# Convolution and locality-gated mixture of experts on one core: weight and token loads in shorter runs, rows that carry 64 channels twice, and one ScalarE copy less a block

## The chip, the cores and the metric

The kernel runs on one core of a Trainium2 chip. The core has a matrix engine (TensorE, "PE" in the profile, with its weight loads as "PEld"), a vector engine (VectorE, "DVE"), an activation engine (ScalarE, "ACT"), a general engine (GpSimd, "POOL") and an engine that mostly issues transfers (SyncE, "SP"). Sixteen DMA engines move data between the main memory (HBM) and the on-chip memory; the profile lists their queues as q0 (transfers that GpSimd issues, which follow index lists), q1 (transfers that SyncE issues) and q8 and q14 (instructions). The metric is the device time of one execution in microseconds (us), as the median of several runs.

## The reference, cut to what matters

Inputs are x with 8 sequences of 3584 tokens of 192 channels, 8 heads with 7 taps, a gate for 8 experts, a local gate, and for each expert two weight matrices (192x1024 and 1024x192). Everything is float32.

```python
w = softmax(weight)                                  # 8 heads x 7 taps
x[b, s] = sum_k w[h, k] * x_pad[b, s + k]            # channels of head h, k = 0..6
logits = x @ w_gate                                  # 8 experts
local = sigmoid(x @ w_local)
for each batch b, for s in order:
    e = argmax(logits[b, s]) if s == 0 or local[b, s] < 0.5 else prev_e
    prev_e = e
    out[b, s] = softmax(logits[b, s])[e] * (relu(x[b, s] @ w1[e]) @ w2[e])
```

So each of the 28,672 tokens goes through the two matrices of one expert, and which expert can depend on the token before.

## The kernel before, in words

The tokens are worked on in 16 parts of 1792 tokens (14 tokens on each of 128 partitions). For every part the kernel computes the convolution, the logits, the expert of each token and the token's place in a table of slots in main memory, sorted by expert. A row of a token in that table (`slots`, one row of `DG` floats) holds the probability, the token's number, its 192 channels and the number once more; that is 195 floats or 780 bytes. GpSimd scatters the rows there (`put`, line 767: one instruction for 128 rows, lines 773 to 776), and once enough rows of an expert stand there, they are read back in blocks.

A block is one or two units of 128 tokens of one expert. There are three kinds, listed in line 882: kind 0 has 35 blocks of one unit, taken while few parts are routed; kind 1 has 87 blocks of two units; kind 2 has 20 blocks of one unit at the end, and two spare ones that run only if needed. The main loop over the blocks (from line 1137) does for block i:

- `ensure` (line 1089) issues the reading of the rows of blocks up to i + 3 (`load_rows`, line 906, tile `xg`, six buffers), and works on the routing of further parts if their rows are not there yet.
- `weights` (line 1100) issues the loads of the expert's two matrices up to block i + 3 (`load_w`, line 896, tile `wb`, four buffers, 1536 KB: 12,288 bytes on each partition). Blocks 0 to 3 load them in three pieces of 512 KB, the others in one DMA.
- `hidden` (line 951) multiplies the first matrix: 48 matmuls with 64 rows each, two row halves of TensorE side by side, into four accumulators `hps`; ScalarE applies the ReLU.
- `turn` (line 927) transposes the rows of block i + 1 on TensorE: 64x128 and, for the last 64 channels, 64x64 pieces. ScalarE then makes four copies from `xps` to `xT`, since each row half of TensorE needs three groups of 64 channels on its own partitions; the last group has to reach both halves.
- `step` (line 1036) puts operations of the next parts' convolution (`conv`, line 366; VectorE and ScalarE) and routing (`route`, line 600) between those of the block, by a budget of time. Routing begins with `logits` (line 564).
- `output` (line 972) multiplies the second matrix, scales on ScalarE and VectorE, and GpSimd scatters the 128 results of each unit to `out` (line 995).

The order on each engine is written out by hand: the program's order is the engines' order. SyncE issues rows, weights and parts' tokens (`load_x`, line 114, tile `x_sb`: 1920 KB, 15,360 bytes on each partition) in one order; a transfer that waits for a buffer, for scatters or for its semaphore holds up those behind it. GpSimd has the scatters to `slots` and to `out` in one order.

The first two parts go another way (`wide`, line 195, and `wide_route`): their convolution is done on TensorE, and GpSimd copies the last 64 channels of the rows aside (`again`, line 221) for the transposes. The rows of the first two blocks are picked on TensorE with a matrix of zeros and ones, `hot` (`hots`, `gather`, `gathered`, lines 546 to 562).

A convolved part lies in `y_sb`, of which there are four buffers (`row_tile`, line 363); `again` and the scatters read it.

Of the kernel before, what the change touches and what calls it, by code (L numbers as in the profile page):

```python
# [8 lines left out]
F32 = mybir.dt.float32  # L9
# [8 lines left out]
P = 128  # L18
B, S, D = 8, 3584, 192
# [4 lines left out]
UT = 128  # L24
# [5 lines left out]
NB = 16  # L30
TB = PT // NB
NI = TB + HALO
NH = NB // 2
NX = NT + HALO
DR = P // 2
# [3 lines left out]
KT = BT // P  # L39
# [18 lines left out]
HALF = 0.5  # L58
FULL = {0: ONE[0], HALF: _sure(PT + PT // 2, UT), **{g: ONE[g] for g in range(1, NPART)}}
REST = NU - ONE[-1] - 2 * TWO[-1]  # L60
DG = 3 + D
Y0 = 2
IX = DG - 1
Q = 32
DQ = D // Q
TQ = (NT + 3) // 4
WA = F * KD // 2
WB = FK * D
# [13 lines left out]
def kernel(  # L82
# [10 lines left out]
    nc = tc.nc  # L93
    cst = ctx.enter_context(tc.tile_pool(name="cst", bufs=1))
# [15 lines left out]

    slots = dram.tile([(DUMMY + 1 + E) * UT, DG], F32, name="slots")


    def load_x(g):
        x_sb = xs.tile([P, NX, D], F32, name="x_sb")
        src = x[g // PER]
        win = bass.AP(tensor=src.tensor, offset=src.offset + g % PER * PT * D,
                      ap=[[NT * D, P], [1, NX * D]])
        nc.sync.dma_start(out=x_sb.rearrange("p t d -> p (t d)"), in_=win)
        return x_sb  # L120

    def load_b(g):
# [15 lines left out]
    with tc.tile_pool(name="scr", bufs=1) as scr:  # L138
        w = scr.tile([1, H, KC], F32, name="w")
# [50 lines left out]
    def z_tile():  # L190
        return yt.tile([P, 3 * NH * TB + NB * DR], F32, name="z")
# [3 lines left out]
    def wide(g, xv, y_sb, both):  # L195
# [25 lines left out]
        def again(half):  # L221
            bs = slice(half * NH, (half + 1) * NH)
            nc.gpsimd.tensor_copy(yr[:, bs, :], y_sb[:TB, bs, Y0 + P:Y0 + D])

        def turned(half, qs):
            at = half * 3 * NH // 2
# [83 lines left out]
    rows = cst.tile([Q, 2, Q], F32, name="rows")  # L310
# [22 lines left out]

    pad = cst.tile([P, DG], F32, name="pad")
    nc.gpsimd.memset(pad, 0.0)
# [17 lines left out]
    def halves():  # L353
        return [(half, slice(half * DR, (half + 1) * DR)) for half in range(2)]

    def turn_half(to, src, half):

        rows = slice(half * DR, (half + 1) * DR)
        nc.tensor.transpose(to, src[rows], identity=ident[rows, rows])  # L359
# [3 lines left out]
    def row_tile():  # L363
        return ys.tile([P, NB, DG], F32, name="y_sb")

# [192 lines left out]
    def gathered(ps):  # L558
        xg = xp.tile([P, KT, DG], F32, name="xg")
        nc.scalar.copy(xg[:, 0, :Y0 + D], ps[:, :Y0 + D])  # L560
        nc.scalar.copy(xg.bitcast(I32)[:, 0, IX:], ps[:, 1:2])
        return xg

    def logits(g, y_sb):

        z = z_tile()[:, :NT * D].rearrange("p (t d) -> p t d", d=D)
        for t in range(0, NT, TQ):
            u = min(t + TQ, NT)
            nc.vector.transpose(z[:, t:u, :], y_sb[:, t:u, Y0:Y0 + D])  # L569
            yield 0.2 * (u - t)  # L570
        yield "hop"


        lps = [hps_p.tile([P, TQ * Q], F32, name="hps") for half in range(2)]
        begin = [min(TQ * j, NT - TQ) for j in range(4)]
        for b in range(DQ):
            for j in range(4):
                for half, rows in halves():
                    nc.tensor.matmul(lps[half][Q * j:Q * j + Q, :], lhsT=wgq[rows, b, :],  # L579
                                     rhs=z[rows, begin[j]:begin[j] + TQ, b * Q:(b + 1) * Q],  # L580
                                     start=(b == 0), stop=(b == DQ - 1))
        ls = sm.tile([P, 2, TQ * Q], F32, name="ls", bufs=1)
        for half in range(2):
            nc.scalar.copy(ls[:, half, :], lps[half])  # L584
        yield "hop"
        lq = sm.tile([P, 2 * TQ, Q], F32, name="lq", bufs=1)
        nc.vector.transpose(lq.rearrange("p t e -> p (t e)"), ls.rearrange("p h x -> p (h x)"))  # L587
        yield 0.4
        lt = sm.tile([P, NT + 2, E + 1], F32, name="lt")
        for r in range(4):  # L590
            for j in range(4):
                t, u = TQ * j, min(TQ * (j + 1), NT)
                at = r // 2 * TQ + t - begin[j]
                e0 = r % 2 * (E + 1)
                nc.vector.tensor_copy(lt[Q * r:Q * r + Q, t:u, :],  # L595
                                      lq[Q * j:Q * j + Q, at:at + u - t, e0:e0 + E + 1])
                yield 0.12
        return lt
# [285 lines left out]
    blocks = [(0, 1, i, next(g for g in FULL if i < FULL[g])) for i in range(ONE[-1])]  # L884
# [3 lines left out]
    AHEAD = 3  # L888
# [7 lines left out]
    def load_w(i):  # L896
        e = entry(i, 1, E - 1)
        wb = wp.tile([P, WA + WB], F32, name="wb")
        src = w12[bass.ds(e, 1)].rearrange("o p x -> (o p) x")

        step = WA + WB if i > AHEAD else (WA + WB) // 3
        for x0 in range(0, WA + WB, step):
            nc.sync.dma_start(out=wb[:, x0:x0 + step], in_=src[:, x0:x0 + step])
        return wb

    def load_rows(i):
        n, group = blocks[i][1], blocks[i][3]
        r = entry(i, 0, DUMMY + 1 - n)
        xg = xp.tile([P, KT, DG], F32, name="xg")
        get = nc.sync.dma_start(  # L910
# [16 lines left out]
    def turn(n, xg):  # L927


        xps = xps_p.tile([P, 2, 512], F32, name="xps")  # L930
        at = xps[:, :, :BT].rearrange("p h (d k s) -> p h d k s", d=2, k=KT)
        for d in range(2):
            for k in range(n):
                src = xg[:, k, Y0 + d * P:Y0 + min((d + 1) * P, D)]
                for half in range(2):
                    turn_half(at[:src.shape[1], half, d, k, :], src, half)
        xT = tp.tile([P, KD, BT], F32, name="xT")
        to = xT.rearrange("p d (k h s) -> p h d k s", k=KT, h=2)
        (_, up), (_, low) = halves()
        for dst, ds, src, d0 in ((slice(0, P), (0, 1), slice(0, P), 0), (low, (1, 3), up, 0),  # L940
                                 (up, (1, 2), up, 1), (up, (2, 3), low, 0)):
            a = to[dst, :, ds[0]:ds[1]]
            b = at[src, :, d0:d0 + ds[1] - ds[0]]
            if n == KT:
                a, b = [v.rearrange("p h d k s -> p h (d k) s") for v in (a, b)]
            else:
                a, b = [v[:, :, :, 0, :] for v in (a, b)]
            copied = nc.scalar.copy(a, b)  # L948
        return xT, copied

    def hidden(n, wb, xT, shares=(1, 1)):
# [100 lines left out]
                time -= c  # L1052

    ya, yb = row_tile(), row_tile()
    hot = cst.tile([P, 2, NB, UT], F32, name="hot")
    wide0 = wide(0, x_in.pop(0), ya, True)
    wide1 = wide(1, x_in.pop(1), yb, False)

# [69 lines left out]
    xT, _ = turn(blocks[0][1], xgs[0])  # L1128
# [8 lines left out]
    for i, (_, n, _, _) in enumerate(blocks):  # L1137
# [6 lines left out]
        if i + 1 < len(blocks):  # L1144
            xT, copied = turn(blocks[i + 1][1], xgs[i + 1])
# [6 lines left out]
    kind, _, at, group = spare[0]  # L1152
    any_left = nc.values_load(tabi[kind, group][at:at + 1, 0:1], min_val=0, max_val=DUMMY,  # L1153
                              skip_runtime_bounds_check_because="an entry of the table")
    with tc.If(any_left < DUMMY):
        for block in spare:
            blocks.append(block)
            i = len(blocks) - 1
            n = block[1]
            xg = load_rows(i)  # L1160
            wb = load_w(i)
            xT, _ = turn(n, xg)
# [3 lines left out]
def _w1_layout(np, w1):  # L1166


    w = w1.reshape(E, KD, DR, 2, F // 2).transpose(0, 3, 2, 1, 4)
    w = np.stack([w[:, 0][:, :, [0, 2, 1]], w[:, 1][:, :, [1, 0, 2]]], 1)  # L1170
    return w.reshape(E, P, KD * F // 2)


# [57 lines left out]
```

## Time and profile before

| What | Value |
|---|---|
| median of 3 runs | 1331.93 us (1331.38 to 1332.31) |
| the profiled execution | 1331.38 us, of it 1329.7 from the first to the last instruction |
| TensorE matmul busy | 1306.9 us, 98% of the span |
| VectorE, ScalarE, GpSimd busy | 778.8, 624.2, 477.9 us |
| moved by DMA | 325.29 MB, 245 GB/s over the span |
| start of block 0, 2, 35 (first block of two units), 122 (first of kind 2) on TensorE | 45.96, 65.23, 264.70, 1213.45 us |

Lines of the profile name the line of the kernel, the engine, the operation, the tile written and the tiles read, the shape and the count; then the busy time, the mean time of one in ns, the engine's idle time before them and what ended that. "issue" there is time for which the profile shows nothing that the engine waited for. In the view by windows the columns are the stretch (us from the span's start), its length, then the busy time of PE, PEld, DVE, ACT and POOL with the number of instructions, the granted clock, the DMA engines' busy share and GB/s. In an engine's order of time the columns are the start, the length, the group and, in brackets, idle time. The slices of the page cut the span into 40 equal parts of 33.2 us, each digit a busy share in tenths.

### The profile page before, as it was taken

How to read it: one execution, taken by the hardware profiler on the slowest of the kernel's cores; microseconds unless marked ns; L12 is line 12 of the kernel's file. 1: busy time of each engine (PE TensorE's matmuls, PEld its weight loads, DVE VectorE, ACT ScalarE, POOL GpSimd, SP SyncE). 2: the span in 40 equal slices, each digit the busy share in tenths (PEclk: the TensorE clock that was granted, in tenths of full speed). 3: DMA queues.
4: the chain of work that ended last, by engine and by line, in shares of the span. 5: the costliest groups of instructions: out<-in, count | busy, mean ns of one | idle time of the engine just before them, and what ended most of it. 6: DMA issues, size and time to landing. Idle time of an engine off the chain costs nothing. (4 is left out here: it accounts for less than half of the span.)

```text
span 1329.7 us, 41356 instructions
## 1 busy us (share of the span) xinstructions
PE 1306.9 (98%) x16682; PEld 1256.0 (94%) x16682; DVE 778.8 (59%) x2434; ACT 624.2 (47%) x1571; POOL 477.9 (36%) x520
## 2 busy tenths in 40 slices
PE   9799999999999999999999999999999999999997
PEld 7799999999999999999999999999999999999997
DVE  5879898977878787878777878786610000000000
ACT  5345555544444544444444444444444444444553
POOL 3445343524243434343434343434344211211111
PEclk9999999999999999999999999999999999999999
DMA  4799999967575757575757575756565555556883
GB/s 184 273 336 386 365 355 353 377 227 264 185 275 185 286 188 280 195 266 191 276 180 276 191 276 191 274 191 217 194 216 207 189 180 188 188 188 232 313 324 123
DMA packets 67298, 325.29 MB, mean 245 GB/s; under 512 B 12576, under 2 KB 38103, under 8 KB 47650
## 3 DMA queue, kind: packets, MB, share of 16 engines
q1 hardware_dynamic: 44784, 277.41, 58.3%
q0 software_dynamic: 22320, 45.22, 9.2%
q8 instruction: 133, 2.18, 0.6%
q14 instruction: 59, 0.48, 0.1%
q10 hardware_dynamic: 2, 0.00, 0.0%
HBM read 277.29 MB, written 45.77 MB: 243 GB/s over the span
## 5 line engine op out<-in xcount | busy, mean ns | idle before, releaser
L979 PE MATMUL yps<-wb,hT 64*128 64x192 f32 x7328 | 641.0, 326 | 5.4 <-DVE o_sb L991 2.7
L962 PE MATMUL hps<-xT,wb 64*128 64x256 f32 (+1 forms) x6816 | 634.1, 336 | 3.3 <-issue 1.8
L979 PEld LDWEIGHTS yps<-wb,hT 64*128 64x128 f32 x7328 | 602.2, 187 | 11.8 <-issue 7.7
L962 PEld LDWEIGHTS hps<-xT,wb 64*128 64x128 f32 x6816 | 581.2, 187 | 33.5 <-issue 4.1
L995 POOL DMA_INDIRECT out_dram<-o_sb,xg x229 | 232.1, 1014 | 604.7 <-DVE o_sb L991 543.7
L967 ACT ACTIVATE hT<-hps 128x512 f32<-128x512 f32 (+1 forms) x568 | 261.6, 512 | 364.4 <-PE hps L962 246.9
L387 DVE SCALAR_TENSOR_TENSOR y_sb<-x_sb,c,y_sb 128x336 f32<-128x336 f32 x672 | 376.3, 570 | 18.4 <-ACT y_sb L377 0.3
L991 DVE SCALAR_TENSOR_TENSOR o_sb<-yps,xg,o_sb 128x192 f32<-128x192 f32 x229 | 87.5, 414 | 468.0 <-ACT o_sb L987 457.7
L774 POOL DMA_INDIRECT slots<-y_sb,posi x228 | 229.0, 1004 | 216.2 <-ACT xT L948 118.8
L987 ACT ACTIVATE o_sb<-yps,xg 128x192 f32<-128x192 f32 x229 | 86.8, 417 | 288.9 <-PE yps L979 283.3
L948 ACT COPY xT<-xps 64x256 f32<-64x256 f32 (+4 forms) x568 | 210.7, 371 | 13.4 <-PE yps L979 1.8
L377 ACT ACTIVATE y_sb<-x_sb,c 128x336 f32<-128x336 f32 x112 | 63.7, 580 | 0.0
L359 PEld LDWEIGHTS xps<-ident,xg 64*128 64x128 f32 (+1 forms) x916 | 54.1, 124 | 5.8
L359 PE MATMUL xps<-ident,xg 64*128 64x64 f32 (+1 forms) x916 | 57.5, 217 | 0.0
L569 DVE STREAM_TRANSPOSE z<-y_sb 128x768 f32<-128x768 f32 (+1 forms) x56 | 45.4, 853 | 0.4
L595 DVE COPY lt<-lq 32x36 f32<-32x36 f32 x224 | 40.7, 182 | 3.5
L579 PE MATMUL hps<-z,wg 64*32 64x128 f32 x1344 | 25.3, 272 | 1.9 <-issue 1.7
L579 PEld LDWEIGHTS hps<-z,wg 64*32 64x32 f32 x1344 | 19.4, 105 | 5.3 <-issue 4.1
L587 DVE STREAM_TRANSPOSE lq<-ls 128x256 f32<-128x256 f32 x14 | 6.2, 441 | 14.2 <-ACT ls L584 14.2
L671 DVE COPY bk<-so_far 1x32 f32<-1x32 f32 x56 | 12.7, 228 | 0.7
L555 PE MATMUL yps<-y_sb,hot 112*128 112x194 f32 x64 | 11.5, 332 | 1.4 <-DVE hot L549 1.4
L555 PEld LDWEIGHTS yps<-y_sb,hot 112*128 112x128 f32 x64 | 10.4, 189 | 2.1 <-DVE hot L549 1.6
(236 smaller groups left out, 358.5 us busy)
## 6 DMA issues: line engine op xcount, KB each, us to landing
wb<-in_w_dram SPq DMA_DIRECT2D x138, 1536.0 KB
x_sb<-in_x_dram SPq DMA_DIRECT2D x14, 1920.0 KB
xg<-slots SPq DMA_DIRECT2D x87, 195.0 KB
wb<-in_w_dram SPq DMA_DIRECT2D x12, 512.0 KB
xg<-slots SPq DMA_DIRECT2D x53, 97.5 KB
out_dram<-o_sb,xg POOLq DMA_INDIRECT x229
slots<-y_sb,posi POOLq DMA_INDIRECT x228
x_sb<-in_xb_dram SPq DMA_DIRECT2D x4, 768.0 KB
```

What stands on the lines that cost most here:

```text
L359: nc.tensor.transpose(to, src[rows], identity=ident[rows, rows])
L377: nc.scalar.activation(cols(h), chans(h, 0), Act.Copy, scale=c[:, h, 0:1])
L387: nc.vector.scalar_tensor_tensor(cols(h), chans(h, k), c[:, h, k:k + 1], cols(h), Alu.mult, Alu.add)
L569: nc.vector.transpose(z[:, t:u, :], y_sb[:, t:u, Y0:Y0 + D])
L774: ins = nc.gpsimd.indirect_dma_start(out=slots[:, :], in_=rows, in_offset=None, out_offset=bass.IndirectOffsetOnAxis(ap=to, axis=0)).ins
L948: copied = nc.scalar.copy(a, b)
L962: nc.tensor.matmul(hps[half][:, j, w], lhsT=wb[rows, f0:f0 + P], rhs=xT[rows, d, w], start=(d == 0 and j == 0), stop=(d == KD - 1), skip_g ...
L967: relu = nc.scalar.activation(hT[:, m:m + 2, w], hps[half][:, :, w], Act.Relu)
L979: nc.tensor.matmul(yps[half][:, k * D:(k + 1) * D], lhsT=hT[rows, m, k * P:(k + 1) * P], rhs=wb[rows, WA + m * D:WA + (m + 1) * D], start= ...
L987: nc.scalar.activation(o_sb[:, k, :], y[k][0], Act.Copy, scale=xg[:, k, 0:1])
L991: nc.vector.scalar_tensor_tensor(o_sb[:, k, :], y[k][1], xg[:, k, 0:1], o_sb[:, k, :], Alu.mult, Alu.add)
L995: sent = nc.gpsimd.indirect_dma_start(out=out, in_=o_sb[:, k, :], in_offset=None, out_offset=bass.IndirectOffsetOnAxis(ap=xg.bitcast(I32)[ ...
```

## The change

The change has two sides.

The first is the size of transfers. `load_w` now loads the weights of all blocks of kind 0 in three pieces of 4096 bytes on each partition, where only blocks 0 to 3 had that; kinds 1 and 2, which came in one DMA of 12,288 bytes on each partition, still do. `load_x` loads a part's tokens in four DMAs of 3840 bytes on each partition in place of one of 15,360.

The second is the row of a token. It now holds the last 64 channels twice: `DG` grows from 195 to 259 floats (1036 bytes). GpSimd makes the second copy, in `again` for the first two parts and at the start of `logits` for the others, and ScalarE makes it in `gathered` for the first two blocks. All transposes in `turn` are then 64x128, and the last 64 channels come out on both halves of the partitions at once. ScalarE needs three copies to `xT` in place of four: one of 128 partitions with two groups, and one of 64 partitions for each half. The first matrix is laid out in another order to match (`_w1_layout`, on the host).

Because rows are longer, the on-chip memory is refitted: `hot` no longer has a tile of its own but takes one of the four `y_sb` buffers.

```diff
-DG = 3 + D
+DG = 3 + D + DR
@@ load_x
-        nc.sync.dma_start(out=x_sb.rearrange("p t d -> p (t d)"), in_=win)
+        to, step = x_sb.rearrange("p t d -> p (t d)"), NX * D // 4
+        for x0 in range(0, NX * D, step):
+            nc.sync.dma_start(out=to[:, x0:x0 + step], in_=win[:, x0:x0 + step])
@@ again
             nc.gpsimd.tensor_copy(yr[:, bs, :], y_sb[:TB, bs, Y0 + P:Y0 + D])
+            nc.gpsimd.tensor_copy(y_sb[:TB, bs, Y0 + D:IX], y_sb[:TB, bs, Y0 + P:Y0 + D])
@@ gathered
         nc.scalar.copy(xg[:, 0, :Y0 + D], ps[:, :Y0 + D])
+        nc.scalar.copy(xg[:, 0, Y0 + D:IX], ps[:, Y0 + P:Y0 + D])
@@ logits
+        nc.gpsimd.tensor_copy(y_sb[:, :, Y0 + D:IX], y_sb[:, :, Y0 + P:Y0 + D])
@@ load_w
-        step = WA + WB if i > AHEAD else (WA + WB) // 3
+        step = WA + WB if blocks[i][0] else (WA + WB) // 3
@@ turn
-                src = xg[:, k, Y0 + d * P:Y0 + min((d + 1) * P, D)]
+                src = xg[:, k, Y0 + d * P:Y0 + (d + 1) * P]
                 for half in range(2):
-                    turn_half(at[:src.shape[1], half, d, k, :], src, half)
+                    turn_half(at[:, half, d, k, :], src, half)
...
-        (_, up), (_, low) = halves()
-        for dst, ds, src, d0 in ((slice(0, P), (0, 1), slice(0, P), 0), (low, (1, 3), up, 0),
-                                 (up, (1, 2), up, 1), (up, (2, 3), low, 0)):
-            a = to[dst, :, ds[0]:ds[1]]
-            b = at[src, :, d0:d0 + ds[1] - ds[0]]
-            if n == KT:
-                a, b = [v.rearrange("p h d k s -> p h (d k) s") for v in (a, b)]
-            else:
-                a, b = [v[:, :, :, 0, :] for v in (a, b)]
-            copied = nc.scalar.copy(a, b)
+        first, by = to[:, :, :2], at
+        if n == KT:
+            first, by = [a.rearrange("p h d k s -> p h (d k) s") for a in (first, by)]
+        else:
+            first, by, to, at = [a[:, :, :, 0, :] for a in (first, by, to, at)]
+        nc.scalar.copy(first, by)
+        for half, rows in halves():
+            copied = nc.scalar.copy(to[rows, :, 2], at[(DR, 0)[half]:(P, DR)[half], :, 0])
@@ main
-    hot = cst.tile([P, 2, NB, UT], F32, name="hot")
+    hot = row_tile().rearrange("p a b -> p (a b)")[:, :2 * NB * UT].rearrange(
+        "p (i b s) -> p i b s", i=2, b=NB)
@@ _w1_layout (host)
-    w = np.stack([w[:, 0][:, :, [0, 2, 1]], w[:, 1][:, :, [1, 0, 2]]], 1)
+    w = np.stack([w[:, 0][:, :, [0, 2, 1]], w[:, 1][:, :, [1, 2, 0]]], 1)
```

## The prediction

> **What bounds the kernel now.** I read the page's engine table and slices first, then PE's groups in three stretches, then PE's order of time, then the packet records of the trace.
>
> ```profile
> PE 1306.9 (98%) x16682; PEld 1256.0 (94%) x16682; DVE 778.8 (59%) x2434; ACT 624.2 (47%) x1571; POOL 477.9 (36%) x520
> DMA  4799999967575757575757575756565555556883
> ...
> q1 hardware_dynamic: 44784, 277.41, 58.3%
> q0 software_dynamic: 22320, 45.22, 9.2%
> q8 instruction: 133, 2.18, 0.6%
> ```
>
> TensorE works in nearly every slice; only slices 3 to 8, the blocks of one unit (kind 0), have the DMA engines full as well. The stretches, in the view by windows (kind 0, two-unit, closing one-unit blocks):
>
> ```profile
> 65.23:264.70 199.47, 195.20 (x3164) 188.87 (x3162) 171.27 (x502) 107.96 (x336) 87.86 (x89) 1.00 0.95 362
> 275.47:1202.91 927.44, 925.95 (x11164) 889.70 (x11163) 542.32 (x1705) 424.29 (x959) 335.94 (x332) 1.00 0.62 219
> 1219.45:1317.46 98.01, 98.01 (x1516) 98.01 (x1515) 7.52 (x18) 50.02 (x162) 17.50 (x18) 1.00 0.81 291
> ```
>
> In the last, 18 blocks follow each other every 5.445 us without a gap. In the first the same kind of block does not. PE, in order of time:
>
> ```profile
> 120.46 1.26 PE L962 MATMUL hps<-xT,wb 64*128 64x128 f32 x16
> 121.95 2.07 PE L962 MATMUL hps<-xT,wb 64*128 64x128 f32 x32 [0.23 <-issue]
> ...
> 1230.34 2.84 PE L962 MATMUL hps<-xT,wb 64*128 64x128 f32 x48
> 1233.01 0.28 PE L359 MATMUL xps<-ident,xg 64*128 64x64 f32 x4
> 1233.13 2.82 PE L979 MATMUL yps<-wb,hT 64*128 64x192 f32 x32
> 1235.78 2.84 PE L962 MATMUL hps<-xT,wb 64*128 64x128 f32 x48
> ```
>
> The block at 120.46 halts mid-way, released by nothing but "issue"; no weight load, ACT or DVE event ends it. PE's idle time by what ended it, blocks 2 to 34:
>
> ```profile
> L962 PEld LDWEIGHTS hps<-xT,wb 64*128 64x128 f32 x1584 | 97.5, 188 | 4.4 <-issue 3.9
> L979 PEld LDWEIGHTS yps<-wb,hT 64*128 64x128 f32 x1058 | 88.3, 187 | 1.6 <-issue 1.3 <-ACT hT L967 0.2
> L579 PEld LDWEIGHTS hps<-z,wg 64*32 64x32 f32 x384 | 6.2, 105 | 4.4 <-issue 4.1 <-PE yps L979 0.2
> ```
>
> Blocks 2 to 34 begin at 65.23 and end at 264.70. Floor: 33 x 5.445 = 179.7, plus four parts' logits at 1.665 each (a two-unit block with logits takes 12.331, one without 10.666) = 6.7. **The excess is 199.5 - 186.4 = 13.1 us**: 6.6 in the four blocks with logits (2.5, 1.9, 1.6, 0.6), 6.2 in nine blocks of 0.5 to 0.9, the rest crumbs.
>
> What is "issue"? q8's 133 packets of 16 KB over 33,678 PE records make 65 bytes each: q8 brings TensorE's program, 256 instructions a packet. I counted the PE records before each packet's start (the trace's packet records). With DMA at ease (936 to 985 us), packet k starts at record 256k + 159 to 188; in the closing blocks at 256k + 179 to 273; in the first stretch at + 185 to 306, and up to 408 around logits. Stalls follow those beyond about 260. A block has 168 instructions in 5.445 us, 32 ns each, so +273 against +159 is 3.7 us late: exactly one weight load's eight 12,288-byte packets on one engine (8 x 462 ns, their median). I read it so: the program packet waits behind one whole weight load.
>
> **The change part by part.** Durations are from the profiled execution, 1331.38 us (span 1329.7 and 1.7 around it), 0.55 below the median of 1331.93.
>
> *Kind 0 weights in three pieces (31 loads more than the first four), tokens in four.* The wait of a program packet falls from 3.7 to 8 x 159 ns (4,096-byte packets) = 1.3 us, 39 instructions: + 200, clear of 260. Nine mid-block halts: between 0 (wrong cause) and -6.2; I take -5, some being other crumbs. Logits: 192 instructions in 1.7 us outrun a prompt packet too; the ten later parts still pay 0.27 each on average (12.33 to 13.51 against 12.331), so four keep 1.1 of 6.6. Between 0 and -6.6; I take -4.5. In the two-unit stretch only token loads are split: its halts sum to some 4 us; between 0 and -4, I take -0.5, the weights there staying whole.
>
> SP issues 62 + 42 DMAs more, 0.53 us apart (57.05 to 58.44, three pieces): 1.07 us a block from SP's 68.1 us of waiting on L979 in 25 waits there, 2.7 each. The eight landing semaphores of SP's DMAs return sooner: a piece waits for the piece two weights before. Those land 4.3 to 11 us before use, and up to eight pieces (1.4 us each) stay queued, so engines aren't starved. 0; with the cover gone, the queue's wait is inside the next term.
>
> [...]
>
> *Longer slot rows (1036 for 780 bytes).* Engine time added in the first stretch, per engine: weights 4192 packets x (3 x 159 - 462 ns) / 16 = 3.9 us; tokens 512 x (4 x 151 - 573) / 16 = 1.0; gathered rows 3840 x 9 ns / 16 = 2.2 (47 ns between the 38 of 780 and the 51 of 1152 bytes); scatters, 52 groups of eight rows x (322 - 247 ns) = 3.9. Sum 11.0 us on 190 busy of 199.5. Weights land 4.3, 5.0 and 4.7 us ahead at blocks 8, 15 and 25 (each behind a token load or a wait for scatters), 7 to 11 elsewhere. If PE gains 4 to 5 us by block 15 and DMA loses 2 to 3, that margin is used up there, and again about block 25. Between 0 and +11; I take +2, nearer to 0 for the reason that follows.
>
> The tightest rows are block 2's (0.99 us before their transposes, but a 2.7 us wait for DVE follows at 61.16) and block 7's (landing 92.41, transposes 94.66). The latter are late because SP waits for scatters, as its queue's waits in the first stretch show:
>
> ```profile
> SPq L910 <- DMA slots<-y_sb,posi: 11.0, 1, 11.0
> ```
>
> The last of them is issued at 82.35 and has landed at 90.5; its packets come in a trickle between the token and weight packets. Behind one load's 1.3 us instead of 3.7 they should land some us sooner, and SP then issues these rows and weights 8 (92.55, the 4.3 us margin) sooner. No loss is taken for block 7 beyond the 1.1 kept above.
>
> *Transposes.* 458 weight loads of 64 columns become 128 wide, 138 instead of 108 ns long. Exposed, (87 x 2 + 55) x 30 ns = +6.9 on each row half; but a 128-column load behind another already steps by 56 ns, the 64-column ones by 55 to 61, which is the 64-element matmul. Between -0.7 (5 ns a block) and +6.9; I take 0. [...]
>
> *ScalarE.* Four copies become three: one-unit 272 + 366 + 2 x 260 to about 380 + 2 x 260, -0.26; two-unit 380 + 577 + 2 x 366 to 595 + 2 x 366, -0.36. They end before the output's matmuls (one-unit 70.07 against 70.71): nothing gained; ACT idles half the time.
>
> *GpSimd.* Four copies of 112x512 at 0.65 us at startup and 14 of 128x896, about 1.2, ahead of logits, before scatters in the same queue. The last startup copy delays the first eight scatters 0.7 us; the ninth waits for DVE until 40.38, 2.2 us after the eighth: covered. Later an output scatter is 1.2 us later, with two o_sb buffers and POOL 36% busy: covered; without cover, 14 x 1.2 = 17. ScalarE's extra 0.2 us copy (gathered) lies before a wait that ends at 42.08. Startup between -0.3 and +0.8: 0. The hot matrix takes a row buffer: conv 3 (from 96.5) now waits for part 0's scatters, the last issued at 52.52, and conv 4 (from 144.4) for part 1's, landed by 114: 0.
>
> Sum: -5 - 4.5 - 0.5 + 2 = -8: 1323.4, and 0.55 for the median: **1324 us**.
>
> **The rivals.**
> 1. *DMA becomes the bound, slower.* Place: blocks 8 to 34. For it: share 0.95, all 16 engines occupied from 93 to 156 us. Packets there took 1.09 of their median, so 11.0 becomes 12; it decides beyond 199.5 - 190 = 9.5 us of addition, if bytes can't move faster. Price: +2.5, plus 2 to 6 for places where the queue is empty today (86 to 92 us, SP waiting for scatters) and for PE's lower clock after such waits (0.95 at 61 us): 1337. Against: 5 us intervals reached 416 GB/s, the mean is 362.
> 2. *Nothing moves.* Program packets wait behind a queue rather than one load, so its cutting doesn't matter, or the halts have another cause; weights still land in time. 1331 to 1333. For it: halts of 0.5 and 0.7 at 53.69 and 54.42, with little DMA traffic.
> 3. *Half of it:* fetches are prompt, but weights take most back: 1328.
>
> **How the numbers follow.** Forecast 0.60, rival 1 0.17, rival 2 0.14, rival 3 0.09. The forecast's own range is 1318 to 1328 (all halts gone and no late weights, against half of them and +2). Half of rival 1, above 1336, and the forecast's lower tail stay outside: 1316 to 1336. A change below 0.2% (2.7 us) can't be told from none. Faster: 0.60 and most of rival 3, 0.68; same 0.15; slower 0.17.
>
> **What would show it.** Right: kind 0 blocks at 5.445 us without "issue" halts, program packets near 256k + 200, two-unit blocks still 10.666, the gain inside 65 to 265 us. Rival 1: PE waiting on DMA wb before L962, DMA share 1.0. Wrong transposes: blocks of 10.7 to 10.8. Wrong: halts kept, or startup later than 65.2 at block 2.

## The result, and the profile after

The changed kernel is slower. Its median is 1338.72 us (four runs, 1336.74 to 1340.35); the kernel before, run beside it, has 1332.12 us (four runs, 1331.38 to 1334.30). The ratio is 1.0046, with a 95% interval from 1.0028 to 1.0064. The forecast was 1324 us, and its range ended at 1336.

The profiled execution of the changed kernel took 1336.74 us, 5.36 more than that of before. Its page, first the busy times, then the slices and the queues:

```profile
PE 1309.3 (98%) x16682; PEld 1259.0 (94%) x16682; DVE 779.4 (58%) x2434; ACT 582.6 (44%) x1431; POOL 491.4 (37%) x538
DMA  5799999977575857575757586756566555556893
...
q1 hardware_dynamic: 59760, 284.88, 59.9%
q0 software_dynamic: 22320, 52.82, 10.4%
q8 instruction: 133, 2.18, 0.6%
```

What the change says it does, it does: q1 has 59,760 packets in place of 44,784, q0 moves 52.82 MB in place of 45.22, and ScalarE is busy 42 us less. These are amounts of work; where the time went is read from the stretches. The three in the view by windows (start and end, length, busy time of PE, PEld, DVE, ACT and POOL, clock, DMA share, GB/s), kind 0, two-unit and closing blocks:

```profile
65.75:268.16 202.41, 196.71 (x3164) 189.43 (x3163) 171.44 (x501) 100.56 (x303) 91.08 (x92) 1.00 1.00 370
278.94:1206.89 927.95, 926.87 (x11164) 891.72 (x11163) 541.42 (x1705) 395.95 (x874) 343.89 (x342) 1.00 0.65 231
1223.43:1321.57 98.14, 98.14 (x1515) 98.14 (x1514) 7.52 (x18) 45.38 (x144) 17.49 (x18) 1.00 0.84 296
```

The first stretch was to lose 7.5 us (the other 0.5 lay in the two-unit blocks) and got 2.9 longer, with the DMA share at 1.00 where it was 0.95. The last tells of the transposes: 18 blocks without a gap in 98.14 us, 5.452 us each, where they were 5.445. Where the 5.2 us of span came from, by the starts of blocks on TensorE:

| Part of the span | before | after | difference |
|---|---|---|---|
| to block 2 | 65.23 | 65.75 | +0.5 |
| blocks 2 to 34 | 199.48 | 202.41 | +2.9 |
| blocks 35 to 121 | 948.75 | 949.28 | +0.5 |
| blocks 122 to 140 | 104.00 | 104.13 | +0.1 |
| block 141 and the end | 12.20 | 13.37 | +1.2 |

The +1.2 at the end is of this one profile: the other profiles of the changed kernel and its variants below have 12.42 (e8, e11) and 12.12 us (e9) there.

The halts that the forecast removed are still there. TensorE's weight loads in blocks 2 to 34, with the idle time ahead of them and what ended it:

```profile
L966 PEld LDWEIGHTS hps<-xT,wb 64*128 64x128 f32 x1585 | 98.2, 188 | 5.2 <-issue 4.9 <-ACT ls L589 0.2
L983 PEld LDWEIGHTS yps<-wb,hT 64*128 64x128 f32 x1058 | 88.7, 187 | 0.6 <-issue 0.4
L584 PEld LDWEIGHTS hps<-z,wg 64*32 64x32 f32 x384 | 6.7, 105 | 7.1 <-issue 6.6 <-PE yps L983 0.2
```

Before, these three groups had 3.9, 1.3 and 4.1 us of "issue"; after, 4.9, 0.4 and 6.6. The logits of block 5 show what such a halt looks like; PE in order of time (start, length, group, idle before):

```profile
88.88 1.21 PE L584 MATMUL hps<-z,wg 64*32 64x128 f32 x36
90.43 0.39 PE L584 MATMUL hps<-z,wg 64*32 64x128 f32 x2 [0.33 <-issue]
91.14 0.29 PE L584 MATMUL hps<-z,wg 64*32 64x128 f32 x1 [0.32 <-issue]
91.86 1.15 PE L584 MATMUL hps<-z,wg 64*32 64x128 f32 x57 [0.43 <-issue]
```

A handful of matmuls, a halt, a handful more, 0.72 us apart, and then the rest at full rate. I use one measure for these from here on, the prediction's own: the **excess** of blocks 2 to 34 is their length less 33 blocks at the kernel's own pace and less 4 x 1.665 us for logits. It is 13.1 us before and 15.8 after. And the **lag** is the number of TensorE records past 256k at which program packet k starts; the forecast was that it falls to about 200. Its mean in that stretch is 267 before and 272 after. That a packet holds 256 records, the lag itself shows: its smallest value in the kernel before is 155 among packets 20 to 59, and 159 among 60 to 99 and among 100 to 130.

### The profile page after: what moved, and what is told of

Its sections match the earlier page's. It is cut to its first block, busy times and chain, and to the rows that moved or that the text cites. A ratio compares the mean times of both kernels' runs of the same rounds, so it can differ in the third digit from the quotient of the medians.

```text
span 1334.9 us, 41576 instructions
## 1 busy us (share of the span) xinstructions
PE 1309.3 (98%) x16682; PEld 1259.0 (94%) x16682; DVE 779.4 (58%) x2434; ACT 582.6 (44%) x1431; POOL 491.4 (37%) x538
## 3 DMA queue, kind: packets, MB, share of 16 engines
q1 hardware_dynamic: 59760, 284.88, 59.9%
q0 software_dynamic: 22320, 52.82, 10.4%
## 5 line engine op out<-in xcount | busy, mean ns | idle before, releaser
L952 ACT COPY xT<-xps 64x256 f32<-64x256 f32 (+1 forms) x284 | 92.2, 325 | 7.0
L950 ACT COPY xT<-xps 128x512 f32<-128x512 f32 (+1 forms) x142 | 72.5, 510 | 4.7 <-PE xps L362 2.0
L362 PEld LDWEIGHTS xps<-ident,xg 64*128 64x128 f32 x916 | 57.8, 138 | 6.1
L362 PE MATMUL xps<-ident,xg 64*128 64x64 f32 x916 | 58.1, 221 | 0.0
L570 POOL COPY y_sb<-y_sb 128x896 f32<-128x896 f32 x14 | 13.3, 951 | 0.0
L558 PE MATMUL yps<-y_sb 112*128 112x194 f32 x64 | 11.5, 331 | 1.8 <-DVE y_sb L552 1.8
```

Source lines behind the costliest of these rows:

```text
L950: nc.scalar.copy(first, by)
L952: copied = nc.scalar.copy(to[rows, :, 2], at[(DR, 0)[half]:(P, DR)[half], :, 0])
```

## The experiments

Fourteen kernels ran, in four sessions. In the two sessions of e1 to e8 the kernel before took 1317.0 us; in the two of e9 to e14, 1331 to 1333, as in the result above. "Occasion" below means one of these two levels of time. The record gives the same chip number for e1 to e11, so the level does not go by that number. Each ratio is to runs of the kernel before in the same session, and profiles are compared within an occasion; each kernel has one profile. Several of the expectations of the first eight name three theories. R is the prediction's: a program packet waits behind one whole load, so shorter runs shorten the lag. E says that the packet waits behind all that is queued, so that only fewer bytes help, and that the longer rows and the wide transposes cost time of their own. B says that the cutting itself costs.

### One side of the change at a time

**e1**, the kernel before with the cut transfers alone:

```diff
+        for x0 in range(0, NX * D, step):                # load_x, step = NX * D // 4
+            nc.sync.dma_start(out=to[:, x0:x0 + step], in_=win[:, x0:x0 + step])
-        step = WA + WB if i > AHEAD else (WA + WB) // 3
+        step = WA + WB if blocks[i][0] else (WA + WB) // 3
```

> The kernel before with the shorter transfers alone (kind 0 weights in three pieces, tokens in four); rows stay 780 bytes, four ScalarE copies. Theory R (the prediction: a program packet of TensorE waits behind one weight load, so pieces shorten the wait): program packets of blocks 2 to 34 start about 200 to 220 records after their 256k, halts gone, 1332 - 8 = 1324 us. Theory E (the wait follows the backlog of the DMA engines, whatever the run size): mean lag stays at 265 to 275 records and the time within 2 us of before, 1330 to 1334. Theory B (the cutting itself costs, by 104 more transfers in SyncE's order and their landing semaphores): most of the 6.6 us that the whole change lost, 1336 to 1339.

Measured: 1318.14 us against 1316.98, ratio 1.0013 (1.0003 to 1.0022). The lag has a mean of 273 records, where the kernel before has 279 on this occasion (e5 below). Cutting alone gains nothing and costs 1.2 us (0.4 to 2.9 by the interval).

**e2**, the changed kernel with the transfers of before (the reverse of that diff):

> The changed kernel with the transfers of before (12,288 and 15,360 byte runs); rows of 1036 bytes, 128-column transposes, three ScalarE copies. Theory R: the rows cost up to 11 us of engine time and nothing is gained, 1334 to 1343. Theory E: the whole loss is here, 1336 to 1340; of it 1.5 us by the blocks' pace (5.452 for 5.445, 10.679 for 10.666 us in the changed kernel's trace), the rest in blocks 2 to 34, at the start and at the end. Theory B: the pace alone, 1333 to 1335.

Measured: 1320.23, ratio 1.0026 (1.0017 to 1.0035). So the side of the rows costs about 3.2 us.

**e3**, e1 with every block's weights in three pieces, two-unit blocks too (`step = (WA + WB) // 3`). In the two-unit stretch without convolution the DMA engines are at ease (share 0.57), and a single load is what a packet can meet there (one is issued every 10.7 us).

> The kernel before with the weights of every block in three pieces and the tokens in four. In the stretch from 936 to 1210 us nothing but weights, rows and outputs is moved, so the lag of a program packet can be read by itself: before it is 159 to 169 records with no load in flight and 226 to 254 when a load of 12,288-byte runs is. Theory R: the upper group falls to about 190 to 200. Theory E: the upper group stays at 230 to 250, as the same bytes are in flight. Time the same as e1 within 2 us by either.

Measured: 1318.35. In that stretch (936 to 1210 us in the kernel before, 15 us earlier here) e5 below has 8 of 24 packets at a lag of 232 to 278 and the rest at 157 to 202, mean 196. With all loads cut, four of 24 lie from 232 up, the largest at 250, but eight between 190 and 226 in place of one, and the mean is 197. By the mean, three times shorter runs bring the packets no sooner. The rest is within the spread of single profiles: e1, whose loads are whole in that stretch, also has only four (of 25) from 232 up, and a mean of 188. The plainer case against R is the first stretch: 273 in e1 and 272 in the changed kernel, where R has 200 to 220.

**e5** is the kernel before and **e8** the changed kernel, run again on this occasion.

> The kernel before, for its profile on this chip. If halts called issue belong to the chip: where e6 and e7 show few of them, this one does too, blocks 2 to 35 taking about 190 us; on a chip like that of the first result about 199 us.

> The changed kernel again, beside e5, e6 and e7 on one chip. Theory E (the longer rows and the wider transposes cost, the cutting next to nothing): the sum of e1 and e2, 4 to 5 us above before if this chip is like that of e1 to e4, 6 to 7 us if it is like that of the first result. Theory B (the cutting costs as much as the rows): 6 us or more on either.

Measured: e5, one run, 1315.65; e8, 1321.25 against 1317.08, ratio 1.0032 (1.0020 to 1.0044). The windows line of blocks 2 to 34 of e5:

```profile
63.00:251.56 188.56, 187.85 (x3164) 185.77 (x3163) 169.35 (x502) 108.50 (x336) 87.89 (x87) 1.00 0.98 381
```

That is 10.9 us less than the same program's 199.5 above, which is most of the 15 us between the occasions. Its excess is 2.2 us, and its lag is no smaller: mean 279, largest 397. So late program packets go with halts on one occasion and without them on the other.

**e6**, the kernel before with 128-wide transposes alone: the second one takes channels 64 to 191, so rows stay at 780 bytes, and ScalarE makes three copies.

```diff
-                src = xg[:, k, Y0 + d * P:Y0 + min((d + 1) * P, D)]
+                src = xg[:, k, Y0 + d * DR:Y0 + d * DR + P]
...
+            copied = nc.scalar.copy(to[rows, :, 2], at[(DR, 0)[half]:(P, DR)[half], :, 1 - half])
```

> The kernel before, rows of 780 bytes, transfers of before, but the second transpose of every unit takes channels 64 to 191 (128 columns) in place of the last 64, which leaves three ScalarE copies as in the changed kernel. If the wider weight loads of the transposes set the blocks' pace: 5.452 and 10.679 us a block and +1.4 to +1.6 us. If the pace came from something else in the changed kernel (longer rows in memory, fewer copies): 5.445 and 10.666 and no change.

Measured: 1319.27, ratio 1.0017 (1.0009 to 1.0026). The blocks run at 5.452 and 10.679 us, exactly the pace of the changed kernel, against 5.445 and 10.666. Twenty two-unit blocks and 18 closing blocks of e6 in the view by windows:

```profile
965.68:1179.26 213.58, 213.58 (x2403) 203.58 (x2402) 14.86 (x40) 82.25 (x180) 54.47 (x56) 1.00 0.56 193
1205.95:1304.09 98.14, 98.14 (x1516) 98.14 (x1515) 7.52 (x18) 45.41 (x144) 17.50 (x18) 1.00 0.82 292
```

The pace is the same on both occasions; times 55 and 87 blocks it is 55 x 0.0075 + 87 x 0.013 = 1.5 us. This version has the benefit of one ScalarE copy less without the longer rows, and is still slower.

**e7**, e2 with the transposes, copies and weight layout of before: the longer rows, the GpSimd copies and the refitted `hot` alone.

> Rows of 1036 bytes, written and read back, GpSimd's copies included, with the transposes, ScalarE copies and transfers of before; the 64 doubled channels are not used. Theory E: e2 less the pace, +1.5 to +2.5 us, of it 0.8 at the start. If the bytes are free and e2's loss was the transposes and the start alone: within 1 us of before with the pace at 5.445 and 10.666.

Measured: 1319.24, ratio 1.0013 (1.0004 to 1.0023), pace 5.445 and 10.666 again, as the same blocks show:

```profile
967.75:1181.07 213.32, 213.32 (x2405) 203.16 (x2403) 14.84 (x40) 89.56 (x200) 54.47 (x56) 1.00 0.58 201
1207.72:1305.73 98.01, 98.01 (x1515) 98.01 (x1514) 7.52 (x18) 50.03 (x162) 17.51 (x18) 1.00 0.84 298
```

Rows alone cost some 2 us. The parts do not add up exactly (1.2 + 2.2 + 2.2 against 4.2), but each is known to about 1.2 us.

### The bytes

**e4**, the kernel before in which blocks 4 to 34 load one third of their weights and use its columns for all:

```diff
+        few = i > AHEAD and not blocks[i][0]
+        step = (WA + WB) // 3 if few else step
-        for x0 in range(0, WA + WB, step):
+        for x0 in range(0, step if few else WA + WB, step):
...
+                    f0 = f0 % ((WA + WB) // 3) if few(i) else f0
```

> The kernel before, in which the blocks 4 to 34 load only the first third of the weights and their matmuls read columns of that third again, so the products of these blocks are left out in part (the same number and sizes of matmuls). DMA share in blocks 2 to 34 should fall from 0.95 to about 0.55. If the halts called issue come from busy DMA engines (R and E alike), blocks 4 to 34 run at 5.445 us apart from logits, program packets start at 160 to 210 records, and the time falls by 6 to 12 us, to 1320 to 1326. If the halts have another cause, the time stays within 2 us of before.

Measured, on the occasion of 1317: 1315.11, ratio 0.9986 (0.9977 to 0.9996), lag 223 in the mean, excess 0.9 us where e5 had 2.2. Fewer bytes shorten the lag (279 in e5), as E has it. The time fell by 1.9 us, where the expectation had 6 to 12 if busy DMA engines make the halts and at most 2 if not; but on this occasion there was little left to gain.

**e11**, the same edit on the changed kernel, fell on the occasion of 1331.

> The kernel after; blocks 4 to 34 load the first third of their weights alone (one DMA of 4096 bytes on each partition) and use its columns again for the rest, so that part of the products in these blocks is not the reference's; the number and the shapes of the instructions on PE stay. The kernel before with the same edit took 0.9986 of before, blocks 2 to 34 in 187.3 us. Theory D: longer rows and the cut transfers cost only by what they add to a full DMA in blocks 2 to 34. With a DMA share near 0.67 that cost is gone, and what is left is the pace of the blocks (1.5 us) and the startup (0.45): blocks 2 to 34 in 187.6 us, two-unit blocks at 10.679, ratio 1.0001. Rival W: the longer rows cost by waits of their own (scatters, buffers, GpSimd's copies ahead of the logits): then the kernel keeps its whole distance to before less the 0.0014 of the same edit: ratio 1.0018, blocks 2 to 34 in 189 us.

Measured: 1338.14 against 1330.95, ratio 1.0053 (1.0033 to 1.0072), beyond both expectations. Blocks 2 to 34 in the view by windows:

```profile
65.66:269.09 203.43, 197.67 (x3165) 189.91 (x3163) 171.03 (x500) 100.95 (x303) 93.08 (x92) 1.00 0.64 215
```

And their weight loads on TensorE:

```profile
L970 PEld LDWEIGHTS hps<-xT,wb 64*128 64x128 f32 x1585 | 98.7, 188 | 5.9 <-issue 5.6
L584 PEld LDWEIGHTS hps<-z,wg 64*32 64x32 f32 x384 | 6.5, 105 | 6.6 <-issue 6.1 <-PE yps L987 0.2
```

The DMA share is 0.64 in place of 1.00, the lag 218 in place of 272, its largest value 324 in place of 369. The stretch is as long as ever, the excess 16.9 us, the "issue" time no less. This takes down E's half on the halts as well as R: on the occasion that has halts, neither the time of the packets nor the load on the DMA engines sets them.

### The startup

**e9**, the changed kernel with the second copy in `again` on ScalarE:

```diff
-            nc.gpsimd.tensor_copy(y_sb[:TB, bs, Y0 + D:IX], y_sb[:TB, bs, Y0 + P:Y0 + D])
+            nc.scalar.copy(y_sb[:TB, bs, Y0 + D:IX], y_sb[:TB, bs, Y0 + P:Y0 + D])
```

> The kernel after, with the second copy of the last 64 channels of the first two parts (four of 112x512) on ScalarE in place of GpSimd. Theory H: at startup VectorE's cast of the places (posi) takes 0.62 us in place of 0.17 because it overlaps GpSimd's second copy, and all behind it comes 0.45 later. Then the cast is at 0.17 again, the first scatter comes 20.75 us after the first convolution matmul (before 20.75, after 21.15 to 21.20), block 0 starts at + 37.1 (before 37.1, after 37.5 to 37.6), and the median is 0.45 us below that of the kernel after: ratio to before 1.0028 where the kernel after has 1.0032. Rival T: block 0 is late by ScalarE's extra copy of the gathered rows or by GpSimd's order; then the cast is short but block 0 stays at + 37.4 or later. Rival A: four copies of about 0.5 us on ScalarE hold up the first parts there; block 0 at + 37.8 or later, ratio 1.0035 or more.

What it tests is visible in the order of time of the changed kernel. First GpSimd, then VectorE (start, length, group):

```profile
26.29 0.74 POOL L225 COPY z<-y_sb 112x512 f32<-112x512 f32 x1 [4.11 <-DVE at L482]
26.98 0.61 POOL L226 COPY y_sb<-y_sb 112x512 f32<-112x512 f32 x1
```

```profile
27.01 0.61 DVE L488 CAST posi<-pos 112x16 int32<-112x16 f32 x1
27.53 0.18 DVE L489 TENSOR_TENSOR y_sb<-pr,rs 112x16 f32<-112x16 f32 x1
```

The cast of the tokens' places, on 16 elements a partition, starts just behind GpSimd's second copy and ends with it. VectorE in the kernel before, and in e9:

```profile
27.03 0.18 DVE L485 CAST posi<-pos 112x16 int32<-112x16 f32 x1
```

```profile
26.81 0.18 DVE L488 CAST posi<-pos 112x16 int32<-112x16 f32 x1
```

Measured for e9: 1335.73 against 1330.95, ratio 1.0042 (1.0026 to 1.0058), too close to the changed kernel's to separate in the time. In the profile, counted from the first convolution matmul: the first scatter at +20.90 us (before 20.75, changed kernel 21.22), block 0 at +38.70 (before 38.45, changed kernel 39.00; the expectation's 37.1 and 37.6 are of the other occasion, where the same step is 0.5). The cast is short again and 0.30 of the 0.55 us is back. The other 0.25 is left. ScalarE's copies (0.63 us for the last one) now run ahead of its own work there, and its extra copy of gathered rows (0.22 us) remains; which of the two it is was not separated. H, the cast behind GpSimd's copy, holds for its part.

### What makes the halts

Three kernels, all from the kernel before, on the occasion of 1331. **e10** shifts TensorE's program against its packets:

```diff
-        awake(7)
+        awake(24, 16)      # 24 warm-up matmuls of 16x16 in place of 7 of 128x128
```

> The kernel before with 24 small matmuls (16x16) in place of seven of 128x128 among those that warm TensorE up at the start: 68 records of PE more ahead of block 0, about 0.4 of a block, and no other difference. Theory S (program supply): the halts follow the place in the 256-instruction program packets; so the halts of the run of before on this chip (0.45 us in block 6, 0.86 in block 16, 0.53 at the logits of block 25) go to other blocks or change by over 0.3 us; the sum of excess in blocks 2 to 34 stays between 0.5 and 4 us, the ratio between 0.999 and 1.0015. Rival F: halts belong to what a block does beside its matmuls (steps of the next part, its semaphores); then the same blocks show them, within 0.2 us.

Measured: 1332.22 against 1330.95, ratio 1.0007 (0.9993 to 1.0021), excess 14.3 us. Outside the blocks with logits, those longer than the pace by 0.3 us or more are 3, 4, 9, 11, 14, 20, 22 and 30, and 2; in the kernel before they are 4, 8, 9, 11, 14, 20, 24, 31 and 33. Five of nine are the same, and the sizes differ by more than 0.2 in some, so this is not F plainly. The expected sum of excess was that of the other occasion, and is not met. But it speaks against S. The program was shifted by 68 records, 0.4 of a block, against its packets; e12 and e13 below, whose code is unshifted and that of before up to block 122, have four and six of before's nine blocks, so the shift changed no more than a repetition does. And halts keep their place in the block. In e10 and the four profiles of that code (before, e12, e13, e14), 57 matmuls of blocks 2 to 34 outside those with logits start late by 0.3 us or more (over the usual step between two such matmuls). Counted in TensorE records from the block's start, all 57 lie in records 0 to 45 or 71 to 106 of some 168; for five the profile names an event as what ended the wait, for four of them, at record 104, ScalarE's `hT`. In the five blocks that e10 shares with before the late matmul stands at record 23 and 17 (block 4), 25 and 21 (9), 31 and 29 (11), 15 and 21 (14), 92 and 94 (20), though the program's packets begin 68 records elsewhere.

**e12** gives VectorE work in the closing blocks: `step` there goes on with

```diff
+        nc.vector.scalar_tensor_tensor(spent["to"][:, :, cols], spent["by"][:, :, cols], c[:, h, 1:2],
+                                       spent["to"][:, :, cols], Alu.mult, Alu.add)
```

> The kernel before; in the closing one-unit blocks VectorE also runs operations of the shape of the convolution's (128x336, about 0.57 us each, some eight a block, on two buffers that nothing else uses then), so that it is about 85% busy there, as in blocks 2 to 34, in place of 8%. Theory V (VectorE's work beside them makes the halts): the closing blocks show them too, by the excess of blocks 2 to 34 of the same run (13 us in 200 us) some 5 to 6 us in their 98 us, or half of that without the logits; the last stretch is 106.5 to 110 us where before has 104.0. Rival: none there, 103.5 to 104.2 us.

Measured, one run: 1340.39 against 1333.07. The closing stretch is 111.7 us, longer than V expected, but not by halts. VectorE is busy 78.8 of 95.35 us from 1230 on, and TensorE's weight loads there have:

```profile
L962 PEld LDWEIGHTS hps<-xT,wb 64*128 64x128 f32 x770 | 48.4, 188 | 0.0
L979 PEld LDWEIGHTS yps<-wb,hT 64*128 64x128 f32 x542 | 46.7, 187 | 6.4 <-ACT hT L967 4.4 <-DVE o_sb L991 1.9
```

The added time is waiting for named events of ScalarE and VectorE. Of "issue", nothing. VectorE's work of this shape does not by itself make the halts.

**e13** has two scatters a block in the closing blocks (`for _ in range(2 if st["block"] > 122 else 1)` around the scatter to `out`).

> The kernel before; in the closing one-unit blocks each block's scatter to the output is issued twice, the same rows with the same values, so that GpSimd issues two scatters a block there in place of one (blocks 2 to 34 have 2.6). Theory G (GpSimd's scatters and the packets that they make are what halts TensorE): the last stretch grows by 2 us or more, to 106 us or more, with halts that end by nothing but issue. Rival: 103.5 to 104.2 us.

Measured, one run: 1367.82 against 1333.07, closing stretch 133.1 us. The weight loads from 1222 to 1345 us:

```profile
L979 PEld LDWEIGHTS yps<-wb,hT 64*128 64x128 f32 x546 | 53.7, 212 | 19.1 <-ACT hT L967 19.1
L962 PEld LDWEIGHTS hps<-xT,wb 64*128 64x128 f32 x838 | 52.1, 190 | 0.0
```

Here the second scatter waits for the first to land, 55.8 us in all of GpSimd's idle time, and TensorE behind it for ScalarE; TensorE's granted clock is 0.93 there. The length is the edit's own doing; halts by issue are absent again, so that G gets no support.

**e14** starts everything later, with 640 warm-up matmuls in place of seven (`awake(640)`).

> The kernel before, with about 205 us of warm-up matmuls more on TensorE at the start (640 in place of 7), so that all blocks come some 200 us later with the same work beside them. Theory L (halts belong to the first quarter of a millisecond of a run, whatever is done): blocks 2 to 34 begin after 260 us and their excess falls from 13 us to 4 or less, so that they take 187 to 191 us. Rival W (they belong to the work): 197 to 202 us, halts in the blocks that had them in before or after (8 to 11, 13 or 14, 20, 30) and in the four with logits.

Measured, one run: 1473.41 us. The warm-up took 142 us more and not 205, so that blocks 2 to 34 run from 204.2 to 408.4 us. Their windows line:

```profile
204.23:408.38 204.15, 197.30 (x3165) 189.85 (x3163) 171.68 (x504) 108.08 (x336) 89.41 (x89) 1.00 0.94 358
```

The excess is 17.8 us, with halts in blocks 3, 8, 10, 12, 22, 24, 30, 33 and others, and in the four with logits. They moved with the work; the time since the start is not their cause.

All profiles side by side (the DMA share is the time of the packets over that of 16 engines, and comes out a little above 1 in places):

| Kernel | before on that occasion | DMA share, blocks 2 to 34 | lag, mean and largest | excess, us |
|---|---|---|---|---|
| before | 1332 | 0.95 | 267, 408 | 13.1 |
| after | 1332 | 1.00 | 272, 369 | 15.8 |
| e9 after, scalar copy | 1331 | 1.00 | 264, 356 | 15.1 |
| e10 shifted | 1331 | 0.96 | 259, 337 | 14.3 |
| e11 after, third of the weights | 1331 | 0.64 | 218, 324 | 16.9 |
| e12, same code as before in this stretch | 1333 | 0.94 | 264, 388 | 16.8 |
| e13, same code as before in this stretch | 1333 | 0.94 | 262, 411 | 17.9 |
| e14 later | 1333 | 0.94 | 258, 338 | 17.8 |
| e5 before | 1317 | 0.98 | 279, 397 | 2.2 |
| e1 cut | 1317 | 1.01 | 273, 389 | 3.9 |
| e2 rows | 1317 | 0.99 | 281, 405 | 3.9 |
| e3 all cut | 1317 | 1.01 | 271, 408 | 4.0 |
| e4 before, third of the weights | 1317 | 0.65 | 223, 333 | 0.9 |
| e6 wide transposes | 1317 | 0.98 | 284, 407 | 3.0 |
| e7 long rows | 1317 | 0.99 | 281, 419 | 5.0 |
| e8 after | 1317 | 1.02 | 278, 408 | 3.7 |

Two readings follow. Within an occasion, a third of the bytes moves the lag by some 55 records and the excess by almost nothing; between occasions the excess changes by 11 us at the same lag. And single profiles of before's code in this stretch differ among themselves, 13.1 to 17.9 us, by more than the 2.7 between before and after. So the +2.9 us of that stretch in the table of the result can't be put down to the change from these two profiles. The calm occasion is the better balance. There the median rises by 4.2 us, and the spans of e5 and e8 differ by 4.0. By the starts of blocks this is 1.8 to block 2, 1.7 in blocks 2 to 34 (0.2 of pace and 1.5 of excess, 3.7 against 2.2), 0.2 in blocks 35 to 121, 0.1 in the closing blocks and 0.2 behind them. Of the 1.8, 1.1 lies ahead of the first convolution matmul (6.24 and 7.30 us), where profiles of before's code range from 6.2 to 7.5 us; 0.5 is the startup told under e9. In blocks 35 to 121 the pace alone would be 1.1; this pair shows 0.2, as e8 happens to have fewer halts there. So a single pair of profiles does not hold the terms apart to better than about 1 us; the pace and the cast are seen by themselves, the rest by the medians of e1, e2 and e7.

No experiment gave a version that beats the kernel before and keeps its result; e4 alone was faster, by leaving weights out.

## Why the prediction was wrong, point by point

**The step that failed** is "I read it so: the program packet waits behind one whole weight load". Every gain rested on it: -5 for mid-block halts, -4.5 for logits, -0.5 in the two-unit blocks. It was a match of two numbers, a lag of 3.7 us and a load's 8 x 462 ns. The lag after is 272 and not 200 (e1 273, e3 unchanged in the mean where the engines are at ease). The step behind it, that stalls follow lags beyond 260, fell too: at a mean of 279 they nearly vanish on one occasion, at 218 they stay on the other. In the kernel before, 11 of 15 packets later than 260 are followed by a late matmul before the next packet, and 4 of the 10 others, which is what the prediction saw; in the changed kernel it is 6 of 16 and 4 of 9, and over the eight profiles of that occasion 59 of 102 and 44 of 97. So the 10 us were not there to be had by cutting the loads, nor by a third of the bytes (e11). The prediction had rival 2 for it (a queue and not one load, or another cause); it was given 0.14, and its evidence, halts of 0.5 and 0.7 us at 53.69 and 54.42 with little DMA traffic, was in the trace and was given little weight. An earlier packet by itself gained nothing: e11 has the lag at 218 in place of 272 and an excess of 16.9 us in place of 15.8. What makes the halts, 13 to 18 us on one occasion, is not shown.

**Longer rows, +2 out of 0 to 11.** The engine time was right: the share rose from 0.95 to 1.00, 202.4 us of work against 190, where the sum of 11.0 gave 201. Its price is of the size taken: e7 costs 2.2 us with the startup in it, e1 1.2 for the pieces. By what wait they cost it is not shown. No group of weight loads in the changed kernel's stretch names a landing of weights as what ended its wait, so rival 1 had the sign and the full DMA engines, but not the mechanism that it named; with the share at 0.64 (e11) the kernel is no faster. That the measured time lies near this rival's 1337 is luck. The clock of 0.95 in rival 1 is a mean from 33 to 66 us; it is 0.5 for 3.4 us from 61.4 on, just behind TensorE's idle 2.7 us up to 61.16, and 1.00 from 64.84 to 1327.77.

**Transposes, 0 out of -0.7 to +6.9.** The term was mis-sized: +1.5 us by the pace of 5.452 and 10.679 (e6 in all 2.2, 1.2 to 3.4 by the interval). The choice went by the step between weight loads (56 ns against 55 to 61), which looks at the loads one by one; what counts is the block, and the prediction itself named 10.7 as the sign of it. Without the 64x64 pieces a two-unit block got 13 ns longer, not shorter.

**ScalarE, 0.** Right: 42 us less busy time, and e6 is no faster for it.

**GpSimd and the startup, 0 out of -0.3 to +0.8.** Wrong by 0.5. The cover was looked for in GpSimd's own queue, the scatters, and there it held. But the copy held up an instruction of another engine, VectorE's cast (0.61 us beside a copy of 0.61; 0.18 in e9, where that copy is on ScalarE), on the chain to block 0. The same shows once more later, in GpSimd's copy ahead of the fourth part's logits. First GpSimd, then VectorE:

```profile
266.29 0.94 POOL L570 COPY y_sb<-y_sb 128x896 f32<-128x896 f32 x1
```

```profile
265.68 2.53 DVE L390 SCALAR_TENSOR_TENSOR y_sb<-x_sb,c,y_sb 128x336 f32<-128x336 f32 x2 [0.50 <-issue]
```

Two such operations take 1.14 us elsewhere (0.57 each); here the first of them took 1.92, at the same copy in the changed kernel on both occasions, and no operation of this kind is over 0.63 in the kernel before. In all six profiles with this copy (the changed kernel, e2, e7, e8, e9, e11) the operation took 1.62 to 1.93 us and ended 0.37 or 0.38 behind the copy. Ten of the other 13 such copies had no VectorE instruction beside them; three had some and held none. In the second case VectorE had started 0.6 us before the copy and was held all the same (a scatter of GpSimd ran just ahead of the copy, and the starts on GpSimd are rough). Of the 18 new copies eight had VectorE work beside them, and two of these held it up; what sets these two apart from the other six is not shown.

**The later terms** stand: gathered rows and weights land in time, the wait of SyncE for scatters at the first part's rows fell from 11.0 to 7.8 us as argued, with no gain from it, and the durations of packets were as taken (4,096 bytes 159 ns, 3,840 bytes 149, 1,036 bytes 47), as was the 1.4 us for a piece of 512 KB: at the startup of the kernel before, pieces ended at 44.44, 45.91, 47.40 and 48.69 us.

## What to carry to other kernels

A stall that ends by "issue" is a wait that the profile does not explain; a matching pair of numbers is a guess at it, and a change that rests on the guess alone should be forecast near zero until one run has moved the supposed cause and seen the stall move. Before an edit spends a resource that is already full (here the DMA engines at 0.95) or adds work to a "free" engine, look at what its neighbours do in that very microsecond (a copy of 0.61 us on GpSimd went with a cast of 0.61 in place of 0.18 on VectorE), not only at its own queue. And a change that touches every block is priced by the block's pace: 13 ns in 87 blocks were worth more than a ScalarE copy that nobody waited for.

## What the runs showed that was not expected

The same program took 1332 us on one occasion and 1317 on another, at a granted clock of 1.00 in blocks 2 to 34 both times; 11 of the 15 us lie in these blocks, and they are "issue" time on TensorE (excess 13.1 against 2.2). The halts come in chains, 0.72 us apart, with a few instructions between. They belong to the work of these blocks (e14), lie at certain places of the block (e10) and are not set by the lag of program packets or DMA load (e11); VectorE's operations alone (e12) and a second scatter (e13) don't bring them into the closing blocks. What does make them stays open. Routing and logits run only ahead of the closing blocks; but ten of the 14 parts have them beside two-unit blocks, where the excess by the same measure is 4.2 us in 949 (2.1 in e5). Leaving them out would have changed which rows every later block holds, so no run here does it.
